# Sinkhorn attention and a residual MLP in one kernel: value mixing beside the token matmuls, its regroup queued behind the residual transposes, gathers on two engines, load gates that wait for all regrouped values, and a TensorE order set by hand

## The chip, the cores and the metric

The kernel runs on one core of one Trainium2 chip. The metric is device time in microseconds (us), the median of several runs. Runs of the kernel before lie between 268.3 and 269.7 us over all rounds, about 0.5% apart; one run took 1457.7 us, is marked slow and is left out. A profile's span (first to last instruction) is about 2 us shorter than the time of the same run. A profile shows one run of its kernel.

Names used below. TensorE (PE in the profile) does matmuls, VectorE (DVE) and ScalarE (ACT) take results out of PSUM, GpSimd (POOL) does elementwise work on SBUF and issues casting loads, SyncE (SP) issues the other DMAs from one queue.

## The reference, cut to what matters

```python
# attention: 4 batches, 8 heads, 768 rows, 64 columns, 8 blocks of 96 rows
P = sort_net                                  # 5 rounds of exp and row/column normalising
k_sorted = einsum('bhij,bhjcd->bhicd', P, k_b)    # blocks of k and v mixed by P
v_sorted = einsum('bhij,bhjcd->bhicd', P, v_b)
attn = softmax(scale * q_b @ k_sb.T)          # inside each block of 96 rows
x = (attn @ v_sb)                             # -> (4, 768, 512)
# residual MLP
tok = einsum('ts,bsd->btd', w_tok, alpha1 * x + beta1)
u   = x + lam * tok
ch  = relu((alpha2 * u + beta2) @ w_ch1) @ w_ch2   # 512 -> 2048 -> 512
out = u + lam * ch
```

Tensor names in the profile: `sc_ps` scores, `et` their exp, `x_ps` attention output, `tok_ps` token mixing, `h_ps` first MLP matmul (`hT` after relu), `ch_ps` second, `v_ps`/`k_ps` value and key mixing, `a2T` the transposed residual that h reads, `u` the residual, `Vs` mixed values in the layout that attention needs, `vscr` the DRAM scratch through which they are regrouped. psA is the PSUM pool with two slots that scores, attention values and mixing share; a matmul group that finds both taken has to wait.

## The kernel before

Each batch is: mix k and v, attention, tok, transpose of the residual, h, ch. The parts that the change and the argument touch:

```python
# value mixing, then the regroup: written to DRAM and read back in another layout, SyncE queue
def mix_v(b, banks=2, groups=range(6), copies=(act.copy, dve.tensor_copy, act.copy)):
    ...                                   # matmuls v_ps, evictions to vA
    for th in range(2):
        nc.sync.dma_start(vscr[b, :, :, th*HB:(th+1)*HB, :]..., vA[th*64:(th+1)*64, :, :])
    for par in range(2):
        regroup[b] = nc.sync.dma_start(Vs[b % NV][par*HB:(par+1)*HB, :, 0:D], vscr[b]...)

def mix_k(b, share=(4, 0, 4), gs=range(3)): ...   # evictions: VectorE all, ScalarE all, VectorE all

def emit_attention(b):
    ...
    prev = [emit_scores(b, 0, g) for g in range(2)]
    for h4 in range(1, H4):
        cur = [emit_scores(b, h4, g) for g in range(2)]
        emit_pv(b, h4 - 1, prev, x128, xs)        # normalise on VectorE
        prev = cur
        if h4 == H4 - 1:
            gather(0, 384)                        # tail rows, all on VectorE
    emit_pv(b, H4 - 1, prev, x128, xs)
    gather(384, C)

def moe_turn(b, hf):                              # residual transposes by DMA, SyncE queue
    for m in range(3):
        nc.sync.dma_start_transpose(uT[:, :, m*128:(m+1)*128], u16[:, 3*hf + m, :])
    for ci in range(CT): dve.tensor_scalar(a2T[hf][:, ci, :], uT[:, ci, :], ...)

# main part, order of TensorE left to the scheduler (priority = program order)
for b in range(1, B):
    if b > 1:
        ...                                       # query transposes of batch 3, on SyncE
        mixing_matrices(b); mix_v(b); ...; mix_k(b)
    emit_attention(b)
    if b == 1: moe_ch(0, 0, (2,))
    else:      moe_h(b - 1, 0); moe_ch(b - 1, 0)
    moe_h(b - 1, 1)                               # reuses the tile hTa
    moe_a(b)                                      # u, tok, residual transposes
    moe_ch(b - 1, 1)
```

The softmax here doesn't subtract the row's maximum and nothing guards it: scores larger than these inputs give would overflow.

## Time and profile before

| | before |
|---|---|
| time | 268.8 us (268.72 to 269.11, 3 runs) |
| span of the profile | 266.8 us |
| head: start to first tok matmul of batch 0 | 34.0 us |
| batch 0 to 1 (first tok to first tok) | 51.3 us |
| batch 1 to 2 | 58.8 us |
| batch 2 to 3 | 58.8 us |
| last stage: first tok of batch 3 to the end | 64.0 us |

From the page of the kernel before: parts 1, 4 and 5 (busy us, share, instructions; then the chain; then groups with busy us, mean ns and idle before).

```profile
span 266.8 us, 5149 instructions
...
PE 257.6 (97%) x2049; PEld 141.6 (53%) x2059; DVE 154.8 (58%) x333; ACT 125.8 (47%) x232; POOL 92.5 (35%) x100
...
PE 89%; ACT 4%; DVE 4%; issue 1%; DMA 1%; DVEq 0%; ACTq 0%
...
L65 PE MATMUL h_ps<-a2T,W1p 128*128 128x384 bf16 x512 | 93.4, 326 | 0.1
```

TensorE looks full. But an h matmul is shown 326 ns long while h matmuls start 163 ns apart, so a busy TensorE is not a TensorE at its peak. To see room, take the distance from each matmul's start to the next one's and compare it with the median of its group (h 163 ns, ch and tok 216, k_ps 56, sc 41, x 29). This "excess" finds stalls that the busy column hides.

From the chain of waits of the kernel before, in order of time (start us, us, what), a stretch inside batch 1 to 2:

```profile
109.28 0.62 PE k_ps L65 x8
109.90 0.02 issue
109.92 0.58 ACT kT L65
110.50 0.01 issue
110.52 0.58 ACT kT L65
111.09 0.01 issue
111.10 0.58 ACT kT L65
111.69 0.01 issue
111.70 0.58 ACT kT L65
```

The second group of key evictions is all on ScalarE, and the chain passes through it for 2.4 us. TensorE was not idle there, it ran h matmuls with gaps.

### The profile page before, as it was taken

To read this page: it belongs to the slowest core of one execution; us is meant where nothing else is said; L and a number is where in the kernel's file an instruction comes from. 1 tells how busy PE (TensorE), PEld (TensorE's weight loads), DVE (VectorE), ACT (ScalarE), POOL (GpSimd) and SP (SyncE) were. 2 spreads that over 40 slices of the span, in tenths; PEclk is the share of its full clock that TensorE was granted. 3 is DMA by queue.
4 is the path that set the end of the run, shared out by engine and by line. 5 is a ranking of instruction groups with operands and counts; after the bars stand their busy time and mean duration, and the time that the engine had idled before them with its cause. 6 is when DMAs were issued, how large, how long until landed. Compare 5 with 4: busy or idle time off the path is not lost.

```text
span 266.8 us, 5149 instructions
## 1 busy us (share of the span) xinstructions
PE 257.6 (97%) x2049; PEld 141.6 (53%) x2059; DVE 154.8 (58%) x333; ACT 125.8 (47%) x232; POOL 92.5 (35%) x100
## 2 busy tenths in 40 slices
PE   7799999999999999999999999999999999999993
PEld 2467745565565444554565444554565445545542
DVE  5878788629567966722585966704675962042033
ACT  3376757643585312980375404970474305504600
POOL 8524689203575615007917225002409000000000
PEclk9999999999999999999999999999999999999999
DMA  6999999999999544499996342494200432012012
GB/s 83 174 208 251 207 210 207 211 216 112 211 157 155 113 84 117 114 82 89 202 211 136 61 100 80 118 98 62 80 2 2 81 76 79 2 39 79 2 39 79
DMA packets 62423, 30.88 MB, mean 116 GB/s; under 512 B 48888, under 2 KB 58112, under 8 KB 62400
## 3 DMA queue, kind: packets, MB, share of 16 engines
q0 software_dynamic: 23024, 15.60, 39.4%
q1 hardware_dynamic: 39280, 14.89, 32.6%
q8 instruction: 16, 0.26, 0.4%
q14 instruction: 7, 0.06, 0.1%
q10 hardware_dynamic: 96, 0.07, 0.1%
HBM read 32.78 MB, written 8.65 MB: 155 GB/s over the span
## 4 chain that ended last, share of the span: by engine, by line
PE 89%; ACT 4%; DVE 4%; issue 1%; DMA 1%; DVEq 0%; ACTq 0%
PE ch_ps L65 31%; PE h_ps L65 30%; PE tok_ps L65 12%; PE x_ps L65 5%; PE sc_ps L65 4%; ACT kT L65 2%; PE v_ps L65 2%; PE k_ps L65 1%; PE q_ps L65 1%; ACT et L65 1%; DVE csum L65 1%; DVE P L65 1%; PE m_ps L65 1%; DVE rsum L65 1%; DMA P<-in_sort_net_dram 1%
## 5 line engine op out<-in xcount | busy, mean ns | idle before, releaser
L65 PE MATMUL h_ps<-a2T,W1p 128*128 128x384 bf16 x512 | 93.4, 326 | 0.1
L65 ACT ACTIVATE hTa<-h_ps 128x384 bf16<-128x384 f32 x96 | 45.9, 492 | 68.1 <-PE h_ps L65 67.0
L65 PE MATMUL ch_ps<-W2p,hTa 128*128 128x512 bf16 (+2 forms) x290 | 65.9, 370 | 0.5
L65 PEld LDWEIGHTS <-W1p 128*128 128x128 bf16 x512 | 47.5, 98 | 30.3 <-issue 0.9
L65 DVE TENSOR_TENSOR ch_ps<-ch_ps,lamB 128x512 f32<-128x512 f32 (+2 forms) x25 | 16.9, 676 | 63.2 <-PE ch_ps L65 60.5
L65 POOL TENSOR_SCALAR u<-b1lB,rs 128x512 f32<-128x512 f32 x18 | 28.8, 1610 | 64.1 <-DVE ost L65 59.3
L65 PEld LDWEIGHTS <-hTa 128*128 128x128 bf16 x300 | 28.7, 98 | 32.4
L65 PE MATMUL tok_ps<-x,w_tokT 128*128 128x512 f16 x144 | 32.1, 379 | 0.0
L65 POOL TENSOR_TENSOR u<-x,u 128x512 f32<-128x512 f16 x22 | 25.3, 1181 | 18.1 <-DVE x L65 17.3
L65 ACT ACTIVATE et<-sc_ps 96x768 f16<-96x768 f32 x32 | 24.9, 807 | 11.7 <-PE sc_ps L65 11.7
L65 ACT CAST u<-u 128x512 f16<-128x512 f32 x24 | 14.8, 618 | 24.8 <-DVE u L65 24.8
L65 PE MATMUL ch_ps<-W2p,hTb 128*128 128x512 bf16 (+2 forms) x100 | 25.0, 371 | 0.0
L65 PEld LDWEIGHTS <-w_tokT 128*128 128x128 f16 x180 | 14.8, 97 | 16.1
L65 DVE TENSOR_TENSOR tok_ps<-tok_ps,a1lB 128x512 f32<-128x512 f32 x24 | 16.5, 692 | 7.3 <-PE tok_ps L65 7.3
L65 DVE CAST kT<-k_ps 64x512 f16<-64x512 f32 x24 | 16.5, 688 | 3.4 <-PE k_ps L65 3.0
L65 DVE TENSOR_TENSOR x<-x_ps,recip 96x512 f16<-96x512 f32 (+2 forms) x32 | 17.6, 554 | 0.9
L65 DVE TENSOR_TENSOR u<-tok_ps,u 128x512 f32<-128x512 f32 x24 | 16.4, 688 | 1.7
L65 ACT ACTIVATE hTb<-h_ps 128x384 bf16<-128x384 f32 x32 | 15.3, 497 | 3.8 <-PE h_ps L65 3.4
L65 DVE TENSOR_TENSOR ost<-ch_ps,u 128x512 f32<-128x512 f32 (+2 forms) x25 | 16.6, 665 | 0.6
L65 POOL DMA_DIRECT2D qn<-in_q_dram x18 | 15.5, 875 | 4.2 <-PE q_ps L65 3.4
L65 PEld LDWEIGHTS <-hTb 128*128 128x128 bf16 x100 | 9.6, 98 | 10.9
L65 PEld LDWEIGHTS <-et 96*128 96x128 f16 (+2 forms) x288 | 12.4, 99 | 4.6 <-issue 1.2
(95 smaller groups left out, 214.7 us busy)
## 6 DMA issues: line engine op xcount, KB each, us to landing
out_dram<-ost SPq DMA_DIRECT2D x23, 192.0 KB, 2.2
raw<-in_v_dram POOLq DMA_DIRECT2D x8, 384.0 KB, 8.9
raw<-in_k_dram POOLq DMA_DIRECT2D x8, 384.0 KB, 10.9
vscr<-vA SPq DMA_DIRECT2D x6, 384.0 KB, 4.4
Vs<-vscr SPq DMA_DIRECT2D x6, 384.0 KB, 7.7
W1p<-in_moe_w_ch_dram POOLq DMA_DIRECT2D x4, 512.0 KB, 10.1
W2p<-in_moe_w_ch_dram POOLq DMA_DIRECT2D x4, 512.0 KB, 17.9
qn<-in_q_dram POOLq DMA_DIRECT2D x12, 128.0 KB, 5.8
```

The source lines that it names most:

```text
L65: ins = getattr(self.eng, name)(*args, **kwargs)
```

## The change

Its intent: keep TensorE fed by an order written out by hand. h and ch matmuls become generators ("fill"), attention becomes a list of steps, and `weave` puts so many microseconds of fill between steps. With it come: value mixing of the next batch beside tok, with the regroup queued behind the residual transposes; tail rows gathered on VectorE and ScalarE; two hT tiles; output written from u in place; a rearranged head without filler ("spin") matmuls between attention steps, with `w_tok` sorted on GpSimd. The loads of batches 2 and 3 wait behind a gate, a tiny GpSimd copy that reads regrouped values, so that GpSimd issues nothing before they have landed. The kernel before has both gates too, but they read one row, which the first of the two reads brings; now they read 32 rows that need both, and the queries of batch 2 are loaded behind the first gate.

```diff
+    def attention_steps(b, first, less=0.0):
+        ...
+        def values(h4):
+            emit_pv(b, h4, ets[h4], x128, xs)
+            if h4 > 1:
+                lo, hi = ((0, 384), (384, C))[h4 - 2]
+                for a in (1, 0, 2):
+                    (dve.tensor_copy if a < 2 else act.copy)(
+                        x128[96:128, a:a + 4:3, lo:hi], xs[32 * a:32 * a + 32, :, lo:hi])
+        yield 0, lambda: scores(0)
+        yield 2.4 - less, lambda: scores(1)
+        yield first, lambda: values(0)
+        yield 2.2 - less, lambda: scores(2)
+        ...
+    def weave(fill, steps):
+        for gap, step in steps:
+            filled = 0
+            while filled < gap:
+                took = next(fill, None)
+                if took is None: break
+                filled += took
+            step()
@@ sorting of w_tok
-            dve.tensor_copy(
+            pool.tensor_copy(
@@ moe_a
+        for kt in range(NT):
+            if ahead and kt < 3:
+                mixes(ahead, kt)                 # value mixing of the next batch
+            tok_part(b, kt)
+            ...
+        if ahead:
+            with tc.issue_after(turned[-1].ins): # behind the residual transposes
+                regroup_v(ahead)
@@ moe_h
-            hTa = moep.tile([128, 12, 384], BF, name="hTa", tag="big", bufs=1)
-            hTb = moep.tile([128, HT - 12, 384], BF, name="hTb", tag="hTb", bufs=1)
+            hT = moep.tile([128, HT, 384], BF, name="hT", tag=("big", "hT1")[hf], bufs=1)
@@ moe_ch: output from u itself, no tile ost
-                dve.tensor_tensor(ost[:, lo:hi], cps[:], u_of[b][kt][:, lo:hi], ALU.add)
+                dve.tensor_tensor(u32[:, lo:hi], cps[:], u32[:, lo:hi], ALU.add)
@@ head
-    mix_v0(0) ... load_weights() ... mix_k0(0); sc0(0, 0, 1) ...
+    load_raw(1, 1)
+    load_w1(range(2))
+    for n in range(3):
+        sort_wtok(n)
+    prep_affine()
+    load_w1(range(2, 4))
+    load_raw(1, 0)
+    for h4 in range(H4):
+        sc0(h4)
+        ...
@@ main part
-    pool.tensor_copy(gate[:], Vs[1][0:1, 0, 0:2])
+    pool.tensor_copy(gate[32:64, :], Vs[1][32:64, 0, 0:2])   # gate: waits for all Vs of batch 1
+    load_raw(2, 1)
+    load_raw(2, 0)
+    load_q(2)
+    cross_q(2, regroup[1])                       # query transposes of batch 2, SyncE queue
+    moe_rows(1, range(5))
+    for b in range(1, B):
+        if b == 1:
+            fill = chain(moe_h(0, 1), moe_ch(0, 0), moe_ch(0, 1, (0,)))
+            steps = [...]
+            steps += attention_steps(1, 8.0, 0.3)
+        else:
+            fill = chain(moe_h(b-1, 0), moe_ch(b-1, 0), moe_h(b-1, 1), moe_ch(b-1, 1, (0,)))
+            steps = [(g, lambda g=g, n=n: mix_k(b, gs=(n,))) for n, g in enumerate((0.6, 3.0, 3.0))]
+            steps.append((3.8, lambda: None))
+            steps += attention_steps(b, 5.3)
+        weave(fill, steps)
+        run(fill)
+        moe_rows(b, range(5, NT))
+        moe_a(b)
+        run(moe_ch(b - 1, 1, (1, 2)))
+        ...                                      # second gate, loads of batch 3, cross_q(3)
```

## The prediction

> What bounds the kernel now. The page gives TensorE 97% busy, and the chain of waits is 89% TensorE (ch_ps 31%, h_ps 30%, tok_ps 12%). The Trainium skill ("Perfetto Trace Analysis", section Identifying the Most-Contended Engine) warns that matmul busy time is a poor measure because matmuls are pipelined. The trace agrees: h matmuls are shown 326 ns long, but start 163 ns apart. So I counted distances between starts in the timeline. Medians: h 163 ns, ch and tok 216, k_ps 56, sc 41, x 29. One steady batch, from the first tok matmul of batch 1 to that of batch 2 (85.4 to 144.2), takes 58.8 us, the next the same. In it h carries about 2.0 us above its median distance and ch 0.5: small stalls, for example the four kT evictions on ScalarE (4 x 0.58 us) that the chain passes through at 109.9. So a steady batch can lose at most about 2.5 us.
>
> Stages, split at each batch's first tok matmul (timeline): head 34.1; batch 0 to 1 51.3; 58.8; 58.8; last stage 63.8 (span 266.8).
>
> What changes.
> - Head. The spin matmuls between attention steps go (10 after 17.5 us, 2.8 us of starts). k and v arrive in head halves, so the first scores need half of k, not all of v and k: they start at 18.1 us now, I expect 14 to 15. But the stretch stays limited by arrivals (about 2 us per half tensor, read from the waits of the issue queue) and by PSUM evictions: per head pair about 2.8 us each on VectorE and ScalarE, against 3.5 of TensorE. sort_wtok moves from VectorE (6 copies, 2.6 us) to GpSimd. The skill ("GPSIMD Engine Reference", section 3.1) has one-input bodies at 1.03 cycles an element; 4608 elements at 1.2 GHz are an estimated 4 us plus overhead, 5 to 6. wt lands about 22.5, so sorted by 28.5, just in time. Six 576-wide evictions on ScalarE then pace the transposes. First tok matmul: 34.1 to about 32.3 (31 to 34.5).
> - Batch 0 to 1. Its excess (about 1.6 us: waits at new ch groups, x and sc groups, unfed v mixing) mostly goes. One ch tile (3.5 us) moves in from behind tok. 51.3 becomes 53.2.
> - Steady batches. Two separate hT tiles let h of half 1 start before ch of half 0 ends; k mixing lies beside h with evictions shared 10 to 2 with VectorE; attention lies over ch, where ScalarE is free. 58.8 becomes 56.9 each.
> - The value regroup behind the transposes has some 20 us of slack; the gather split moves only work off TensorE's path.
> - Last stage: loses the moved ch tile and about 0.3: 63.8 becomes 60.0.
>
> Sum: 32.3 + 53.2 + 56.9 + 56.9 + 60.0 = 259.3 span; plus the 2 us by which time exceeds span, 261.5 us. Range 257.5 to 265.5. Faster by over 2%: 0.70; within 2%: 0.27; slower: 0.03.
>
> What would show it. Right: first scores by 15 us; tok starts near 32.3, 85.5, 142.4, 199.3; no h or ch excess over 1 us in a steady batch. Wrong: TensorE waiting on sorted wt (GpSimd slow or blocked in its DMA queue), on psA slots (exp or normalise), or on transposes before h.
>
> What would make it wrong. The fixed TensorE order turns each late eviction into a stall instead of letting other work pass; gaps of 2.2 to 2.4 us against 1.7 us of exp plus relus on ScalarE are tight. The head may gain nothing if GpSimd copies take twice my estimate, or k and q of batch 1 land late (expected 44 to 49, needed 47 to 49). It could be better if the head is bound by TensorE alone: then 29 to 30.

## The result

The changed kernel took 264.83 us (264.74 to 265.04, 4 runs) against 268.89 (268.72 to 269.11): a ratio of 0.985 (95% interval 0.983 to 0.987). Ratios here and below are the mean time of one kernel's runs over that of the other's of the same rounds, so not quite the ratio of the medians. Executions over 1.5% slower than the fastest of the same kernel are left out of the means. The gain is 1.5%, inside the range that I gave, but in the class "within 2%", not in the one that I held likelier. I expected 7.3 us and got 4.1.

| stage (us) | before | predicted | after | after less predicted |
|---|---|---|---|---|
| head | 34.0 | 32.3 | 32.5 | +0.2 |
| batch 0 to 1 | 51.3 | 53.2 | 56.9 | +3.7 |
| batch 1 to 2 | 58.8 | 56.9 | 57.3 | +0.4 |
| batch 2 to 3 | 58.8 | 56.9 | 55.9 | -1.0 |
| last stage | 64.0 | 60.0 | 60.4 | +0.4 |
| span | 266.8 | 259.3 | 263.0 | +3.7 |

One stage holds the whole difference. (One ch tile, 3.5 us, moved from the last stage into batch 0 to 1, so the rows before and after do not show each stage's gain.) The page of the changed kernel, the same lines:

```profile
span 263.0 us, 5120 instructions
...
PE 250.5 (95%) x2047; PEld 140.2 (53%) x2047; DVE 146.4 (56%) x323; ACT 132.7 (50%) x240; POOL 93.4 (36%) x101
...
PE 70%; DMA 14%; POOL 7%; DVE 5%; issue 2%; ACT 0%; SPq 0%; DVEq 0%; POOLq 0%
...
L65 PE MATMUL h_ps<-a2T,W1p 128*128 128x384 bf16 x512 | 89.0, 326 | 0.8 <-DVE u L65 0.7
```

The share of TensorE in the chain fell from 89 to 70%: DMA and GpSimd are now on it. Who made TensorE wait, from the waits view of the changed kernel, TensorE only (waiter, releaser: us in total, times, longest); these are the three longest waits behind the first tok:

```profile
PE tok_ps L65 <- DVE x L65: 1.1, 1, 1.1
PE h_ps L65 <- DVE u L65: 0.7, 1, 0.7
PE k_ps L65 <- DMA raw<-in_k_dram: 0.6, 1, 0.6
```

In distances between starts these are 1.31 us at 87.9 before the first tok of batch 1, 0.86 us at 107.9 in h of batch 1, and 0.77 us at 47.3 before the key mixing of batch 1. Stage 2 to 3 has no excess above 0.1 us at all: there the woven order does what it was made for.

The wait at 107.9 comes a long way. The SyncE queue of the changed kernel, in order of time (start us, us of issue, what):

```profile
37.35 1.49 SPq L361 DMA_DIRECT2D vscr<-vA  x2
48.20 11.37 SPq L366 DMA_DIRECT2D Vs<-vscr  x2
78.39 8.71 SPq L140 DMA_TRANSPOSE qT<-qn  x6
87.20 0.53 SPq L729 DMA_DIRECT2D out_dram<-u  x1
...
94.14 10.86 SPq L650 DMA_TRANSPOSE a2T<-u  x6
```

GpSimd in the same stretch (in brackets the idle time before it, and what ended it):

```profile
66.41 0.18 POOL L65 COPY gate<-Vs 32x2 f16<-32x2 f16 x1 [23.13 <-DMA Vs<-vscr]
...
75.61 7.74 POOL L65 TENSOR_SCALAR u<-b1lB,rs 128x512 f32<-128x512 f32 x5
89.98 1.57 POOL L65 TENSOR_SCALAR u<-b1lB,rs 128x512 f32<-128x512 f32 x1 [6.64 <-DMA out_dram<-u]
91.52 6.78 POOL L65 TENSOR_TENSOR u<-x,u 128x512 f32<-128x512 f16 x6
```

And VectorE just before the wait ends:

```profile
106.25 1.25 DVE L65 TENSOR_SCALAR a2T<-a2T,ab2col 128x384 bf16<-128x384 f16 x4 [2.83 <-DMA a2T<-u]
107.42 0.69 DVE L65 TENSOR_TENSOR ch_ps<-ch_ps,lamB 128x512 f32<-128x512 f32 x1
108.14 0.69 DVE L65 TENSOR_TENSOR u<-ch_ps,u 128x512 f32<-128x512 f32 x1
```

Read together: the values of batch 1 land at 66.4 us, which opens the gate; the queries of batch 2 load; their transposes sit in the SyncE queue from 59.6 and are issued at 78.4 to 87.1. The outputs of batch 0 stand behind them. The first output tile is ready at 75.9 and is written at 87.2; the next two, ready at 80.9 and 84.5, follow it. Since output now goes out of u itself, the sixth u of batch 1 needs that buffer, and GpSimd waits 6.6 us for it. Its adds end at 98.3, the residual transposes at 105.0, VectorE scales their second half at 106.3, and only then frees the PSUM bank that h needs. Each link is in the trace; whether taking one away helps is for experiments.

### The profile page after: what moved, and what is told of

It is laid out like the page before. It is cut to its first block, busy times and chain, and to the rows that moved or that the text cites. A ratio compares the mean times of both kernels' runs of the same rounds, so it can differ in the third digit from the quotient of the medians.

```text
span 263.0 us, 5120 instructions
## 1 busy us (share of the span) xinstructions
PE 250.5 (95%) x2047; PEld 140.2 (53%) x2047; DVE 146.4 (56%) x323; ACT 132.7 (50%) x240; POOL 93.4 (36%) x101
## 4 chain that ended last, share of the span: by engine, by line
PE 70%; DMA 14%; POOL 7%; DVE 5%; issue 2%; ACT 0%; SPq 0%; DVEq 0%; POOLq 0%
PE h_ps L65 29%; PE ch_ps L65 28%; DMA wt<-in_moe_w_tok_dram 7%; PE tok_ps L65 6%; DMA raw<-in_k_dram 6%; PE sc_ps L65 2%; PE x_ps L65 2%; POOL u L65 2%; POOL wtp L65 2%; PE k_ps L65 1%; POOL raw L65 1%; DMA a2T<-u 1%; DVE u L65 1%; DVE a2T L65 1%; DVE ch_ps L65 1%
## 5 line engine op out<-in xcount | busy, mean ns | idle before, releaser
L65 PE MATMUL h_ps<-a2T,W1p 128*128 128x384 bf16 x512 | 89.0, 326 | 0.8 <-DVE u L65 0.7
L65 ACT ACTIVATE hT<-h_ps 128x384 bf16<-128x384 f32 x128 | 60.4, 492 | 55.7 <-PE h_ps L65 55.2
L65 PE MATMUL ch_ps<-W2p,hT 128*128 128x512 bf16 (+2 forms) x400 | 86.9, 371 | 0.0
L65 PEld LDWEIGHTS <-hT 128*128 128x128 bf16 x400 | 37.6, 98 | 41.0
L65 POOL TENSOR_TENSOR u<-x,u 128x512 f32<-128x512 f16 x22 | 25.3, 1185 | 28.9 <-DVE x L65 28.7
L65 PE MATMUL tok_ps<-x,w_tokT 128*128 128x512 f16 x144 | 32.9, 379 | 1.1 <-DVE x L65 1.1
L65 DVE CAST kT<-k_ps 64x512 f16<-64x512 f32 x30 | 20.6, 687 | 5.5 <-PE k_ps L65 5.1
L65 DVE RECIPROCAL recip<-x_ps 96x8 f32<-96x8 f32 (+1 forms) x32 | 6.2, 195 | 30.1 <-PE x_ps L65 30.1
L65 DVE TENSOR_TENSOR u<-ch_ps,u 128x512 f32<-128x512 f32 (+2 forms) x25 | 16.7, 669 | 0.8
L65 POOL DMA_DIRECT2D qn<-in_q_dram x16 | 14.0, 908 | 3.8 <-DMA raw<-in_v_dram 3.0
L65 PEld LDWEIGHTS <-et 96*128 96x128 f16 (+1 forms) x288 | 12.0, 105 | 2.8 <-DVE xs L65 0.3
L65 PE MATMUL x_ps<-Vs,et 96*128 96x65 f16 (+1 forms) x288 | 12.8, 197 | 0.2 <-DVE xs L65 0.2
```

Source lines behind the costliest of these rows:

```text
L65: ins = getattr(self.eng, name)(*args, **kwargs)
```

## The experiments

Twelve runs. TensorE, VectorE, ScalarE and GpSimd have the same instructions in the same order up to the first tok, compared by operation and operand, in the variants that leave the head alone, yet their profiles put that first tok anywhere from 32.5 to 33.9 us. So stage lengths tell more than spans, and the changed kernel was run again as a control.

### 1. Query transposes behind the first output

```diff
-    cross_q(2, regroup[1])
@@ moe_ch, after the two writes of a tile
+                if (b, kt) == (0, 0):
+                    cross_q(2, written)
```

> Only the place of the six query transposes of batch 2 in the SyncE queue changes: behind the first output tile of batch 0 instead of in front of all of them. Theory A (head-of-line: the transposes wait from 59.6 to 78.4 us for their queries and hold the outputs, so the seeds u of batch 1, tile 5, wait for a buffer until 90 us, GpSimd's adds end at 98.3, the residual transposes at 105, and h of batch 1 waits 0.86 us at 107.9): GpSimd's 6.6 us wait for out goes, its adds end 1 to 2 us earlier, the h wait at 107.9 goes, stage 1 to 2 falls from 57.3 to about 56.4, time 264.8 to 264.0. Rival B (the residual transposes are late because tok itself is late, by the 1.3 us wait on VectorE before it): adds end where they did, the h wait stays, time 264.8.

Measured: 264.67 us (264.18 to 264.81, 4 runs), ratio to before 0.984. Stages 33.4, 56.2, 57.1, 55.9, 60.4. GpSimd in this run:

```profile
76.53 9.29 POOL L65 TENSOR_SCALAR u<-b1lB,rs 128x512 f32<-128x512 f32 x6
89.95 6.78 POOL L65 TENSOR_TENSOR u<-x,u 128x512 f32<-128x512 f16 x6 [4.13 <-DVE x L65]
```

The wait for the output is gone, as theory A said, and the adds end 1.6 us earlier, at 96.7. But they now wait for x from VectorE; the residual transposes still end at 104.9, and an h wait of 0.63 us stays. The time is that of the changed kernel. Neither theory alone holds. (Experiment 9 shows how far the h wait varies without this edit: 0.63 us is no change.)

### 2. Value steps of batch 1 earlier

```diff
-            steps += attention_steps(1, 8.0, 0.3)
+            steps += attention_steps(1, 6.0, 0.3)
```

> One number: in batch 1 the first value step comes after 6.0 instead of 8.0 us of filling, so about 2 us more of ch matmuls are left behind the last value step. Theory A (tok of batch 1 waits 1.3 us because the last normalise and tail gathers are still running when the filling has run out): the wait before tok falls from 1.3 to under 0.3, stage 0 to 1 from 56.9 to about 55.8, time to about 263.8. Rival B (VectorE is simply full in this stretch, so whatever is moved makes another wait): the 1 us comes back as waits of scores and values on psA slots, time 264.8. Both fail if Vs of batch 1 (landed 66.4) were not yet there: it is, the value step would come at about 70.5.

Measured: 263.39 us (262.74 to 264.36, 4 runs), ratio 0.980 (0.977 to 0.982). Stages 33.0, 54.35, 58.9, 55.9, 60.4. The tok wait went altogether and stage 0 to 1 fell by 2.6 us, more than expected; 0.8 of it is the wait for keys, which is absent here but also in the control (experiment 9), against which the stage fell by 1.8. But stage 1 to 2 grew by 1.6: an h wait of 2.14 us at 106.1. The profiled run is the slowest of the four, 1.0 us above the median, so this wait is probably shorter in the others. GpSimd, then VectorE, in this run:

```profile
90.02 1.56 POOL L65 TENSOR_SCALAR u<-b1lB,rs 128x512 f32<-128x512 f32 x1 [6.76 <-DMA out_dram<-u]
91.56 6.78 POOL L65 TENSOR_TENSOR u<-x,u 128x512 f32<-128x512 f16 x6
...
92.75 0.69 DVE L65 TENSOR_TENSOR u<-tok_ps,u 128x512 f32<-128x512 f32 x1 [3.21 <-POOL u L65]
```

x was ready 2 us sooner, but GpSimd was still held by the output write, at the same 90.0 us as before. Most of what tok gained was handed back at the next release. Theory A holds for tok; the return comes from what the first experiment moved, not from psA slots as rival B had it.

### 3. Keys of batch 1 before the last quarter of W1

```diff
-    load_w1(range(2, 4))
-    load_raw(1, 0)
+    load_w1(range(2, 3))
+    load_raw(1, 0)
+    load_w1(range(3, 4))
```

> The keys of batch 1 are issued before the last quarter of W1 instead of after it. Theory A (the wait of 0.77 us at 47.3 for these keys is a place in the DMA line behind GpSimd's sorting): keys land about 2 to 3 us earlier, the wait goes, and time falls by 0.5 to 0.8 us, to about 264.2, unless the last quarter of W1, now 3 to 4 us later at about 50, is missed at 54. Rival B (the wait only passes on to the queries of batch 1, which land at 49.9): time unchanged, a wait of similar size at the first query transposes.

Measured: 265.15 us (264.66 to 265.61, 4 runs), ratio 0.986. Inconclusive. The wait for keys is gone, and no later one took its place (W1 was in time), but that wait is also absent from the first and second experiments and from the control, which load the keys in the old place; it is there with 0.35 us in experiment 11. It comes and goes with the arrival of loads.

### 4. The hand-set order undone

```diff
 def weave(fill, steps):
     for gap, step in steps:
-        filled = 0
-        while filled < gap: ...      # fill taken
         step()
@@ main part
-    pe.fixed = True
+    pe.fixed = False
```

> Undo of the hand-set order alone: in batches 1 to 3 all attention steps are emitted first and the filling after them, and TensorE's order is left to the scheduler, as in the kernel before; two hT buffers, the value mixing beside tok and all else stay. Theory A (the gain of the steady batches comes from the woven order): stages 1 to 2 and 2 to 3 go back to about 58.5, stage 0 to 1 grows too, time about 267 to 269. Rival B (the gain comes from the second hT buffer, the eviction shares and the value mixing beside tok): stages stay at 56 to 57.5, time within 0.5 us of 264.8.

Measured: 275.39 us (273.72 to 275.6, 4 runs), ratio to before 1.022 (1.018 to 1.026): slower than the kernel before. Stages 33.1, 62.1, 59.6, 58.3, 60.3. The steady batches fall back by 2.3 and 2.4 us, close to the 58.8 of before, and stage 0 to 1 loses 5.2. From its waits view, TensorE:

```profile
PE x_ps L65 <- DMA Vs<-vscr: 4.6, 1, 4.6
```

Theory A holds: the woven order is where the steady gain comes from (no clock loss enters there: in both steady stages the granted clock was 1.00). It also hides the late values of batch 1: in the hand-set order the first value step comes after 66.4 us, here it came at 61.4 and waited. I expected at most 269; the miss is this wait and some matmuls after it that start at half rate (the granted clock of stage 0 to 1 was 0.94).

### 5. Both first edits together

> Both first edits together. Each alone moved one release and met the other: with the transposes moved, GpSimd's adds still began at 89.95 us because x was late; with the values earlier, tok began at 87.3 but the adds still began at 91.6 because tile 5 of u waited for its buffer. Theory A (two serial causes, each hiding the other): together tok starts near 87.4, adds begin by 88 and end by 95, no h wait over 0.3 us near 104 to 108; stages 54.4 and 56.0 to 56.3; time 261.0 (260.5 to 261.8), which beats both kernels. Rival B (the residual transposes are bound by their own queue, so the gain of the earlier tok is given back as in the run with the values earlier): stage 1 to 2 about 58.5, time 263.4.

Measured: 262.98 us (262.33 to 264.12, 5 runs), ratio 0.979 (0.977 to 0.982). Stages 33.8, 54.35, 56.7, 55.9, 60.4. GpSimd and SyncE:

```profile
84.00 1.76 POOL L65 TENSOR_SCALAR u<-b1lB,rs 128x512 f32<-128x512 f32 x1 [0.32 <-DMA out_dram<-u]
87.87 6.77 POOL L65 TENSOR_TENSOR u<-x,u 128x512 f32<-128x512 f16 x6 [2.11 <-DVE x L65]
...
91.88 10.24 SPq L650 DMA_TRANSPOSE a2T<-u  x6
```

| | first tok of batch 1 | GpSimd's adds | residual transposes issued by | h wait | stage 0 to 1 | stage 1 to 2 |
|---|---|---|---|---|---|---|
| after | 89.45 | 91.5 to 98.3 | 105.0 | 0.86 | 56.9 | 57.3 |
| 1: transposes moved | 89.60 | 90.0 to 96.7 | 104.9 | 0.63 | 56.2 | 57.1 |
| 2: values earlier | 87.34 | 91.6 to 98.3 | 104.5 | 2.14 | 54.35 | 58.9 |
| 5: both | 88.16 | 87.9 to 94.6 | 102.1 | 0.26 | 54.35 | 56.7 |

In the traces theory A holds: two causes in series, each hiding the other. With both, the two stages take 111.0 us together, against 113.2 to 114.2 in the profiles without either edit (the changed kernel and experiments 3, 9 and 11), so 2.1 to 3.2 us less. By time alone this run can't be told from experiment 2: the ratios are 0.979 and 0.980 with the same interval. What the first edit adds to the second is shown by the table, not by the clock. The expected 261.0 was missed by 2 us; 1.3 of it is this run's late head, the rest lies in stage 1 to 2, which I had put at 56.0 to 56.3.

### 6. The regroup in front of the residual transposes

```diff
+            if ahead and kt == 2:
+                regroup_v(ahead)
             if kt % 3 == 2:
                 moe_rest(b, kt)
-                moe_turn(b, kt // 3)
-        if ahead:
-            with tc.issue_after(turned[-1].ins):
-                regroup_v(ahead)
+                with ExitStack() as behind:
+                    if ahead:
+                        behind.enter_context(tc.issue_after(regroup[ahead].ins))
+                    moe_turn(b, kt // 3)
```

> Undo of the named part: the value regroup of batches 2 and 3 is written and read on the SyncE queue in front of the residual transposes instead of behind them. Theory A (the queue is served in order and the read waits for the write to land, about 5 us, plus 2.4 us of issue): residual transposes end 7 to 8 us later in batches 1 and 2, h of the next batch waits 4 to 6 us each time, time 272 to 277. Rival B (transfers run side by side and the order in the queue is of no weight): time within 0.5 us of 264.8.

Measured: 295.27 us (294.21 to 296.89, 4 runs), ratio 1.100. Stages 33.8, 56.2, 77.4, 64.7, 60.4. TensorE in time order:

```profile
112.54 1.72 PE L65 MATMUL h_ps<-a2T,W1p 128*128 128x384 bf16 x4 [6.90 <-DVE a2T L65]
...
129.95 4.79 PE L65 MATMUL h_ps<-a2T,W1p 128*128 128x384 bf16 x16 [9.48 <-ACT hT L65]
```

The direction is theory A's, the size is three times it. h waits 6.9 us for the first half of the transposes. The second half comes later still: the early regroup opens the gate at 109.7, and the loads of batch 3 now run beside the transposes. The last three of these land 7 to 12.5 us after their issue, where in the changed kernel they take 2.4; in batch 2, with no loads beside them, they take 2.4 here too. VectorE waits 11.8 us for them with evictions behind, and h 9.5 us. After both waits h matmuls start 320 ns apart instead of 163, for about 4.3 us each time; most of the second line is such matmuls. The Trainium skill ("TensorE: Matmul & The Clock Gate", Part 1) says that the array's clock is halved to 1.2 GHz after an idle window of about 3.4 us, until it has been busy for as long; this trace agrees on the halving, 384 columns at 1.2 GHz being 320 ns, and shows a somewhat longer recovery. Summed over the two stages, the half-rate matmuls cost 5.2 of the 28.9 us, by their distances; nearly all the rest is waits. So in front of the transposes is the wrong place. The kernel before did not have it there either (it wrote the values of batch 2 at 109.3, after its residual transposes had been issued by 99.3), so this run does not say what the change gained.

### 7. Tail rows gathered on VectorE alone

```diff
-                    (dve.tensor_copy if a < 2 else act.copy)(
+                    dve.tensor_copy(
```

> Undo of the named part: all tail rows gathered on VectorE, none on ScalarE. Theory A (VectorE is the engine that releases tok in batch 1): wait before tok of batch 1 grows from 1.3 by 0.3 to 0.7 us, other batches have filling enough and stay, time 265.0 to 265.5. Rival B (the gather is off every path): time 264.8 and the same stages within 0.1.

Measured: 266.57 us (265.73 to 267.22, 4 runs), ratio 0.992. Stages 33.6, 57.1, 57.05, 55.9, 60.3. The excess before the first tok of batch 1 is 1.88 us, with 0.42 more before the value mixing in front of it, against 1.31 in experiment 6, which is the same up to there: 1.0 us more. Steady batches do not move. Theory A holds; my size was low, and I had the gather off TensorE's path. The profiled run is the fastest of the four; the median lies 1.7 us above the changed kernel's, so 1.0 us may be low. From its waits view:

```profile
PE tok_ps L65 <- DVE x L65: 1.7, 1, 1.7
```

### 8. Without the first gate

```diff
-    pool.tensor_copy(gate[32:64, :], Vs[1][32:64, 0, 0:2])
     load_raw(2, 1)
```

> Undo of the named part, first of the two gates: the loads of batch 2 no longer wait for the regrouped values of batch 1 (which landed at 66.4 us, with the DMA engines at 9 tenths until then). Theory A (the gate protects the regroup's read from 3 MB of loads): Vs of batch 1 lands after 72 us, the first value step, at 72.5, waits 1 to 4 us, time 266 to 269. Rival B (the gate delays the queries of batch 2, whose transposes hold the outputs until 87 us; without it they are done by about 75): GpSimd's wait for out and the h wait at 107.9 go, time 263.5 to 264.3.

Measured: 272.05 us (270.72 to 273.39, 4 runs), ratio 1.013. Stages 32.9, 65.4, 57.0, 55.9, 60.4. Its waits view, TensorE:

```profile
PE x_ps L65 <- DMA Vs<-vscr: 4.8, 1, 4.8
```

The query transposes were issued at 72.7 instead of 78.4, as rival B said, but the values landed at 78.5 instead of 66.3, 5 us too late for the first value step: theory A outweighs it, by more than the 266 to 269 us that I gave. The granted clock of the run fell to 0.98, and 1.7 of the 8.5 us in this stage is eight ch matmuls that start 426 ns apart after the wait. The gate earns its place. It is no gain of the change, though: the kernel before has it as well, on one row.

### 9. The changed kernel again

No edit.

> The changed kernel itself, unedited, as a control. Profiles with an identical head put the first tok matmul anywhere from 32.5 to 33.8 us, and runs of this kernel's variants spread over 0.5 to 1.5 us, against 0.3 of the record. If the head moves with the arrival of loads, time is 264.7 to 265.5, tok at 32.5 to 33.8 and all stages behind it as before (56.2 to 56.9, 57.1, 55.9, 60.4); then the variants were compared with too low a number. If the head is fixed, time is 264.8 and tok at 32.5.

Measured: 264.38 us (263.79 to 264.91, 5 runs), ratio 0.984 (0.982 to 0.986). Stages 32.7, 56.2, 57.9, 55.9, 60.4. The waits before tok (1.31 us) and in h (here 1.49) are there again, the wait for keys is not. The same kernel's stage 1 to 2 differs by 0.6 us between two profiles: where tok comes earlier, h waits longer. That is the release at about 108 us seen in experiment 2, without any edit. Over the profiles that leave both causes in place (the changed kernel and experiments 3, 7, 9 and 11) this h wait lies between 0.2 and 1.5 us. The time is a little below the 264.7 to 265.5 that I expected.

### 10. w_tok sorted on VectorE

```diff
-            pool.tensor_copy(
+            dve.tensor_copy(
@@ from before the attention of batch 0 to just before the transposes
-    for n in range(3):
-        sort_wtok(n)
```

> Undo of one part of the head: the six sorting copies of w_tok go back to VectorE, just before the transposes. Theory A (GpSimd gives VectorE room while attention of batch 0 runs; the copies took 2.6 us on VectorE): transposes start about 2 us later, first tok at 35 or later, time plus 1.5 to 2.5 us. Rival B (the head is bound by the landing of w_tok at 23.6 and the 4.8 us on GpSimd behind it; on VectorE the copies are done by 26.5, and W1 and the keys of batch 1 are issued 5 us sooner): tok at 31 to 32.5, the wait for keys at 47.3 goes, time minus 0.5 to 1.5.

Measured: 267.52 us (267.46 to 268.55, 4 runs), ratio 0.996. First tok at 36.1; the other stages as in the control. Its waits view, TensorE:

```profile
PE wtok_ps L65 <- DVE wtp L65: 2.1, 1, 2.1
```

Theory A holds for the place that I chose, the end of attention. The kernel before had the copies between attention steps; that place was not tried. On GpSimd the six copies took 4.8 us after the landing at 23.6. I had estimated 5 to 6 from the 1.03 cycles an element of the Trainium skill ("GPSIMD Engine Reference", section 3.1). The trace nearly agrees: up to 1.20 us for 1152 elements, the total just under the range.

### 11. One hT tile from batch 1 on

```diff
-tag=("big", "hT1")[hf], bufs=1)
+tag=("big", "hT1")[hf if b == 0 else 0], bufs=1)
```

> Undo of one part of the steady batches: from batch 1 on both halves share one hT tile, as before; only batch 0 keeps two. Theory A (my prediction: two tiles let h of half 1 start before ch of half 0 ends): stages 1 to 2 and 2 to 3 grow by 1 us or more. Rival B (the hand-set order already puts h of half 1 behind ch of half 0, so the second tile matters only in batch 0): these stages stay within 0.2 us of 57.1 and 55.9, the last within 0.4 of 60.4, time within 0.5 us of the control.

Measured: 265.11 us (264.56 to 265.66, 4 runs), ratio 0.986. Stages 33.9, 56.5, 56.65, 55.9, 60.3. The steady stages are no longer than in the control. The time is 0.7 us above the control's, more than the 0.5 that I allowed, but this profile's head is 1.2 us later. Rival B holds: in the steady batches the second tile does nothing, because the hand-set order has h of half 1 behind ch of half 0.

### 12. Experiments 1, 2 and 3 in one kernel

> The two edits that worked together plus the keys of batch 1 before the last quarter of W1. Theory A (only the head's arrivals and the key wait are left): stages behind the first tok 54.0 to 54.4, 56.7, 55.9, 60.4; time 262.2 to 263.0, below the 263.0 of the two edits or equal to it. Rival B (the last quarter of W1 now lands too late): an h wait near 54 us, time above 263.2.

Measured: 262.36 us (262.07 to 263.22, 5 runs), ratio to before 0.977 (0.974 to 0.979), against 0.984 (0.982 to 0.986) for the unedited change in the same rounds. Stages 33.6, 54.35, 56.75, 55.9, 60.4. It beats both kernels. From experiment 5 it can't be told apart, so what the third edit adds is not shown.

## Why the prediction was right or wrong

- What bounds the kernel, and how much a steady batch can lose: right. I said at most about 2.5 us of 58.8. Stage 2 to 3 lost 2.8; of this 0.43 is value mixing (two matmuls of 216 ns) that now falls before the stage's first tok instead of inside it. Experiment 4 gives 2.3 and 2.4 us back: the order is the cause. Nearly half of it works in a way that I had not named. Each passage (a switch, below) of TensorE between 128-row matmuls and the 64-row scores or a 32-row matmul costs about 0.1 us. A steady stage has 18 of them before (1.9 us of excess, with one stall of 0.3 among them), 8 after (0.8 us), because the scores now come in groups of sixteen, and 16 again in experiment 4.
- One reason for it was wrong: "Two separate hT tiles let h of half 1 start before ch of half 0 ends". Experiment 11 shows no effect in these batches.
- Head: right, 32.3 predicted, 32.5 and 32.7 in the two profiles of this kernel. The first scores came at 14.6 us (14 to 15 predicted), sorting ended at 28.5. That it is "limited by arrivals" fits the spread up to 33.9 for the same instructions, but no run shows which arrival.
- Batch 0 to 1: this is the step that failed, "Its excess ... mostly goes ... 51.3 becomes 53.2". It measured 56.9, and that is the whole miss of 3.7 us. Experiment 2 is 2.6 us shorter: the tok wait, 1.3 us, a wait of 0.3 in the last value step, and the wait for keys, 0.8, which its edit does not touch and which is not in every run. I had checked psA slots and late loads, not whether enough fill was left behind the last value step to cover its normalise and gather. In batches 2 and 3 there were 13 ch matmuls left (2.8 us), in batch 1 only 6 (1.3 us), and tok waited about that difference. This is the danger that I had named in general, a fixed order that "turns each late eviction into a stall"; I had looked for it in the wrong place.
- The other 1.1 us remain even without waits (54.35 against 53.2). In the stage I count 18 excesses of 92 to 108 ns, 1.7 us in all, each where TensorE goes from full-height h or ch matmuls to 64-row scores, half-width query transposes or the 32-row matmuls of the mixing matrices, or back. The Trainium skill ("TensorEngine Tiling (Array Packing)", Key Properties) says that changing the tiling mode drains the engine; the places agree. The kernel before has 21 of them in this stage, 2.2 us by the same count. So the excess that I expected to go "mostly" was in large part switches, and the woven steps of this batch keep nearly all of them. No experiment takes them away, so this part is counted and not tested.
- "The value regroup ... has some 20 us of slack": right that no value step of batches 2 and 3 waits for it, too large in size. Of batch 2 the values landed by 120.0 and were first read at 127.5, of batch 3 at 175.8 and 183.8: 7.5 and 8 us. Its place in the queue matters more than its slack (experiment 6). "The gather split moves only work off TensorE's path": wrong in batch 1, where it is worth 1.0 us (experiment 7).
- What I named as dangers: "transposes before h" did come, through a path that I had not seen, from the SyncE queue to GpSimd's buffer (experiments 1, 2 and 5). "k and q of batch 1 land late" came in some runs, by up to 0.8 us.

Left open: what decides the head's spread, whether removing the switches of batch 0 to 1 would give back the remaining 1.1 us, and where a better place for the sorting in the head is.

## What to carry to other kernels

When the order is set by hand, check at the end of each woven stretch that the fill left over covers the longest tail of evictions there. A DMA that waits in a queue holds everything behind it, also writes whose buffers another engine needs: put it behind what is ready earlier. When an edit takes a wait away and the time stays, look for a second release at the same instant before giving the edit up; here two edits gave 0.2 and 1.4 us alone, and 1.9 together, by medians whose runs scatter by about 1 us; only the waits in the traces made the case for both.

## What the Trainium skill lacked or had wrong

- "DMA: Bandwidth & Descriptors" has the order in which queues start and complete transfers, but I found nothing there on what an issue that waits for its data costs those behind it. Here six transposes that waited 18.8 us for their queries held three finished output tiles until 87.2 us or later, the first for 11.3 us.
- The same page (Latency and other measured facts) gives 261 GB/s for a DMA transpose, measured on another kernel. Here the issue set the rate: six transposes of 131 KB each (128 x 512, two bytes) kept the queue 8.3 to 8.7 us, 90 to 95 GB/s, 1.2 us an issue.
- "TensorEngine Tiling (Array Packing)" says that a mode switch drains the engine, with no figure. Here a switch cost 92 to 108 ns, each way, as the excess over the median distance.
- "GPSIMD Engine Reference" (section 3.1) has no figure for a tensor-scalar operation with one scalar per row: 512 f32 elements took 1.56 us here, more than the 1.19 us of a two-input add of the same size.
